# A long convolution beside an MLP: the filter in the inputs' time layout, gate weights ahead of a convolution input, and a resplit opening

## The chip, the cores and the metric

The program runs on 1 core of one Trainium2 chip. Times are device microseconds (us) of that core; the lower, the better. Every kernel was timed several times, beside runs of the kernel before on the same chip. All runs compared here are fast ones (granted clock 0.998 to 1.0).

## The reference

The output and all gradients of one layer, with S = 2048, D = 1024, F = 3584, in bf16:

```
xn  = layernorm(x)                                  # x is A_q
kv  = shift4(k) * v                                 # 4 taps along time
y   = irfft(rfft(kv, 2S) * rfft(h, 2S))[:S]         # h is ssm_k [D, S]
out = x + xn * (y + kv * ssm_D) + (relu(xn @ Wg) * (xn @ Wu)) @ Wd
returns out and the nine gradients, for a given grad_out
```

## The kernel before

TensorE is the engine that everything waits for. Most of its work is the MLP: matmuls of 128x512, each starting 0.216 us after the last. The convolution ("branch A") works on 8 groups of 128 channels. Its pieces are dealt out into the MLP's stream of matmuls: every 1760 ns of TensorE work there is a slot, and in each slot a generator of the branch may put in one piece for TensorE, with ScalarE copying the result, and one for VectorE.

Of a group, the parts that matter here are these. The gradient times xn (`gt`) and the filter (`hn`) each get their first Fourier step. `gt` comes in time layout: partition 64u + q, row r holds time 32q + 16u + r. The filter comes by channels, so TensorE transposes it first; 16 transposes take every 16th time step:

```python
    def h_tile(self, st):
        hT = self.ttile("hT")
        hv = st["hn"][:].rearrange("p r c -> p (r c)").rearrange("p (q r) -> p r q", r=16)
        pst = self.ps.tile([P, 16, P], BF16, name="pst", tag="aps")
        for r in range(16):
            self.pri.now()
            self.pri.pin(self.nc.tensor.transpose(pst[:, r, :], hv[:, r, :], self.identA[:]))
        self.act(hT[:, 0:16, :], pst[:])
        return hT
```

Here the two halves of time (u) are interleaved over the partitions, so the first Fourier step of the filter needs a table of its own, RH, of which half the entries are zeros:

```python
    def fwd1_filter(self, st, hT):          # the filter: 4 slots of 2 matmuls, full height
        ...
        for r0 in range(0, NB1, 8):
            for jj in range(2):
                r = r0 % 16 + 4 * jj
                self.mm(ps[:, 512 * jj:512 * jj + 512], self.RH[:, r0 // 16]..., hT[:, r:r + 4, :]...)
            self.act(B[:, :, r0:r0 + 8, :], ...)
            yield

    def fwd1(self, st, key, src):           # all other inputs: 2 slots of 4 matmuls, 64 rows each
        ...
        for r0 in range(0, 16, 8):
            for j in range(r0, r0 + 8, 4):
                for u in range(2):
                    rows = slice(64 * u, 64 * u + 64)
                    self.mm(ps[:, u]..., self.R[rows]..., src[rows, j:j + 4, :]...)
                self.act(B[:, :, :, j:j + 4, :], ...)
            yield
```

The loads of the branch's first group, and the slots in which it begins (`yield n` lets n ns of TensorE work pass; a slot is a pair of what goes to TensorE and to VectorE):

```python
    def steps(self):
        ...
        yield 13000
        self.load_xn(nx)       # xt: xn in time layout, from xn_d in DRAM, in pieces of 256 bytes
        self.load_taps(nx)     # skb
        self.pin = False
        yield 9000
        self.pri.strict = True
        hT = self.h_tile(nx)
        ...
    def slots(self, st, hT, gi):
        ...
        yield f1h, (lambda: self.gate_grad(st)) if gi == 0 else None     # gt = gt * xt
        yield f1h, tk
        yield f1h, self.both(lambda: self.add_D(st), tk)
        yield f1h, tk
```

The opening normalizes x in chunks of 1, 1, 1, 1, 2, ... tiles of 128 rows, so chunk 4 holds tiles 4 and 5. ScalarE sums the rows and the squares, VectorE subtracts and scales, TensorE transposes a tile into PSUM (the buffer that its results land in), VectorE copies it out as `xnT`, and the gate matmuls of that tile can start. 24 warm-up matmuls come before. The loads are issued by one queue, in this order:

```python
    load(4)
    first.append(b.row_block_T(B_W_down, 0, "wdT", 2))
    goT = [b.load_T(g, i, "goT", 8 + i) for i in range(2)]   # transposing loads
    load(5)                                                 # layer-norm chunk 5: tiles 6 and 7
```

## Time and profile before

| | before |
|---|---|
| time, median of 3 runs | 1922.31 us (1921.58 to 1922.76) |
| profiled execution | 1920.26 us, span 1918.5 us, clock 1.0 |
| TensorE busy | 1909.4 us of the span, 100% when rounded |
| VectorE, ScalarE busy | 47%, 33% |
| TensorE's waits named by the profile | about 5 us in all, 1.6 of them for gate weights |

The lines that this rests on stand in the prediction below. As there, costs are taken from the start of one block of matmuls to the start of the next, not from printed durations.

### The profile page before, as it was taken

What the parts mean: (1) busy time and instruction counts of PE and PEld (TensorE: products, weight loads), DVE (VectorE), ACT (ScalarE), POOL (GpSimd) and SP (SyncE); (2) the same over time, 40 slices, a digit from 0 to 9 for tenths busy, and PEclk for the clock granted to TensorE, in tenths of its full rate; (3) what the DMA queues carried; (4) which work ended last, traced back from release to release, by engine and by line L of the source; (5) the groups of instructions that cost most, each with busy time, mean ns of one, the idle gap of its engine ahead of it and who ended that gap; (6) DMA issues with size and microseconds to landing.
All of it is one profiled execution on the core that took longest, in us unless ns stands there. A gap on an engine that the chain in (4) does not pass through costs nothing.

```text
span 1918.5 us, 36320 instructions
## 1 busy us (share of the span) xinstructions
PE 1909.4 (100%) x15582; PEld 886.9 (46%) x15582; DVE 910.2 (47%) x1364; ACT 635.8 (33%) x867; POOL 15.7 (1%) x38
## 2 busy tenths in 40 slices
PE   9999999999999999999999999999999999999999
PEld 4444444444444444444444444444444544444444
DVE  6767767767777754534444354310122232222222
ACT  5854354364364354354344344321000000000000
POOL 1100000000000000000000000000000000000000
PEclk9999999999999999999999999999999999999999
DMA  9975778974874982645663633385999964554553
GB/s 249 276 179 144 178 185 183 221 189 133 186 187 134 248 225 78 175 128 183 158 163 92 170 100 122 100 203 209 257 240 254 235 157 121 121 121 121 121 121 72
DMA packets 628002, 323.16 MB, mean 168 GB/s; under 512 B 458360, under 2 KB 597376, under 8 KB 627840
## 3 DMA queue, kind: packets, MB, share of 16 engines
q1 hardware_dynamic: 617344, 299.99, 64.1%
q10 hardware_dynamic: 9216, 16.65, 2.9%
q0 software_dynamic: 1280, 4.20, 0.7%
q8 instruction: 122, 2.00, 0.4%
q14 instruction: 40, 0.33, 0.1%
HBM read 143.79 MB, written 95.44 MB: 125 GB/s over the span
## 4 chain that ended last, share of the span: by engine, by line
PE 96%; DVE 1%; ACT 1%; DMA 1%; issue 0%; POOL 0%; SPq 0%; ACTq 0%; POOLq 0%
PE ps_x L1283 20%; PE ps_w L1056 20%; PE ps_o L1214 10%; PE ps_h L805 9%; PE ps_u L805 9%; PE ps_g L805 9%; PE ps_d L1056 9%; PE ps L72 7%; PE ps_d L1069 1%; PE ps_w L1069 1%; ACT ln_j L743 1%; PE ps_warm L851 0%; PE pst L308 0%; PE ps_r L1244 0%; DMA wg<-in_B_W_gate_dram 0%
## 5 line engine op out<-in xcount | busy, mean ns | idle before, releaser
L1056 PE MATMUL ps_w<-ugs,xn_nat 128*128 128x512 bf16 x1728 | 383.9, 379 | 0.0
L805 PEld LDWEIGHTS <-xnT 128*128 128x128 bf16 x1792 | 170.2, 98 | 212.0 <-issue 10.2
L1056 PEld LDWEIGHTS <-xn_nat 128*128 128x128 bf16 x1728 | 164.9, 98 | 199.4 <-issue 5.5
L805 PE MATMUL ps_g<-wg,xnT 128*128 128x512 bf16 x896 | 207.0, 379 | 3.2 <-DMA wg<-in_B_W_gate_dram 1.6
L1301 ACT ACTIVATE w<-xn,m 128x512 f32<-128x512 bf16 x32 | 24.3, 806 | 553.0 <-issue 317.2
L805 PE MATMUL ps_u<-wu,xnT 128*128 128x512 bf16 x896 | 207.0, 379 | 0.5 <-ACT gh L975 0.4
L805 PE MATMUL ps_h<-wdT,goT 128*128 128x512 bf16 x896 | 206.1, 379 | 0.0
L1283 PE MATMUL ps_x<-wgT,ggT 128*128 128x512 bf16 x896 | 198.6, 379 | 0.0
L1283 PE MATMUL ps_x<-wuT,guT 128*128 128x512 bf16 x896 | 198.6, 379 | 0.0
L1214 PE MATMUL ps_o<-wd,hT 128*128 128x512 bf16 (+1 forms) x896 | 187.6, 372 | 0.0
L1056 PE MATMUL ps_d<-g_nat,hs 128*128 128x512 bf16 x768 | 172.1, 379 | 0.0
L1283 PEld LDWEIGHTS <-guT 128*128 128x128 bf16 x896 | 87.7, 98 | 105.7
L1283 PEld LDWEIGHTS <-ggT 128*128 128x128 bf16 x896 | 87.7, 98 | 105.5
L1214 PEld LDWEIGHTS <-hT 128*128 128x128 bf16 x896 | 87.7, 98 | 99.9
L805 PEld LDWEIGHTS <-goT 128*128 128x128 bf16 x896 | 85.2, 98 | 102.6 <-issue 2.9
L319 DVE STREAM_TRANSPOSE flp<-C 128x1024 f32<-128x1024 f32 x48 | 90.5, 1930 | 83.4 <-ACT C L76 83.4
L908 DVE SCALAR_TENSOR_TENSOR ru<-ru,ps_u 128x512 bf16<-128x512 bf16 x112 | 76.5, 683 | 108.6 <-issue 43.3
L975 ACT CAST gh<-ps_h 128x512 bf16<-128x512 f32 x112 | 65.4, 585 | 164.1 <-PE ps_h L805 154.8
L1160 ACT CAST wi<-ps_w 128x512 bf16<-128x512 f32 x108 | 63.6, 589 | 161.8 <-PE ps_w L1056 150.1
L76 ACT CAST C<-ps 128x1024 bf16<-128x1024 f32 x96 | 92.5, 1015 | 69.1 <-PE ps L72 68.1
L319 DVE STREAM_TRANSPOSE flp<-B 128x1024 f32<-128x1024 f32 x48 | 90.8, 1939 | 48.6 <-ACT B L76 48.6
L1056 PEld LDWEIGHTS <-hs 128*128 128x128 bf16 x768 | 72.7, 98 | 88.9 <-issue 4.2
(175 smaller groups left out, 1482.6 us busy)
## 6 DMA issues: line engine op xcount, KB each, us to landing
ug_d<-ru SPq DMA_DIRECT2D x112, 256.0 KB, 3.6
ugs<-ug_d SPq DMA_DIRECT2D x112, 256.0 KB, 4.4
wg<-in_B_W_gate_dram SPq DMA_DIRECT2D x56, 256.0 KB, 4.7
wu<-in_B_W_up_dram SPq DMA_DIRECT2D x56, 256.0 KB, 4.8
h_d<-ht SPq DMA_DIRECT2D x112, 128.0 KB, 3.6
hs<-h_d SPq DMA_DIRECT2D x56, 256.0 KB, 5.1
out_dram<-wi SPq DMA_DIRECT2D x56, 256.0 KB, 2.5
gt<-in_grad_out_dram SPq DMA_DIRECT2D x32, 256.0 KB, 4.0
```

Source lines behind the costliest of these rows:

```text
L72: self.pri.pin(self.nc.tensor.matmul(out, lhsT=lhsT, rhs=rhs, start=start, stop=stop))
L76: self.pri.pin(self.nc.scalar.copy(out=out, in_=in_))
L319: self.pri.pin(self.nc.vector.transpose(out=df[:, c0:c0 + 32, :], in_=sf[:, c0:c0 + 32, :]))
L805: self.pri.pin(self.nc.tensor.matmul(ps[:], lhsT=xT[:, kt * P:(kt + 1) * P], rhs=w(kt), start=(kt == 0), stop=(kt == self.DT - 1)), always ...
L908: self.pri.pin(nc.vector.scalar_tensor_tensor(out=ru[s][:, 1, :], in0=ru[s][:, 0, :], scalar=0.0, in1=ps[:], op0=ALU.is_gt, op1=ALU.mult))
L975: self.pri.pin(nc.scalar.copy(out=gh[:], in_=ps[:]))
L1056: self.pri.pin(self.nc.tensor.matmul(ps[:], lhsT=lhsT(st), rhs=rhs(st), start=(st == 0), stop=(st == self.ST - 1)))
L1069: self.pri.pin(self.nc.tensor.matmul(ps[i][:], lhsT=lhsT(i, st), rhs=rhs(i, st), start=(st == 0), stop=(st == self.ST - 1)))
L1160: self.pri.pin(nc.scalar.copy(out=wo[0][:, d, :], in_=ps[:]))
L1214: nc.tensor.matmul(ps, lhsT=hT[:, kt, :], rhs=self.wd[:, kt, oc], start=(kt == 0), stop=(kt == self.FT - 1))
L1283: nc.tensor.matmul(ps, lhsT=T[:, kt, :], rhs=W[:, kt, oc], start=(i == 0), stop=(i == n - 1))
L1301: nc.scalar.activation(out=w[:, oc], in_=xn[:, oc], func=ACT.Identity, scale=m[:, 7:8], bias=m[:, 6:7])
```

## The change

It has three intents. **The filter in the time layout of the other inputs**: with time half u on partitions 64u to 64u+63, the filter's first Fourier step can use `fwd1` and the table R, in 2 slots rather than 4, and RH with its zeros goes. For that, each transpose becomes two of 64 weight columns. **Gate weights ahead of xt** in the DMA queue, since TensorE had been waiting for them, with the first reader of xt moved to a later slot. **The opening split over ScalarE and VectorE**, with fewer warm-up matmuls.

```diff
@@ h_tile
-        hv = st["hn"][:].rearrange("p r c -> p (r c)").rearrange("p (q r) -> p r q", r=16)
+        hv = st["hn"][:].rearrange("p r c -> p (r c)").rearrange("p (q u r) -> p u r q", u=2, r=16)
         for r in range(16):
-            self.pri.pin(self.nc.tensor.transpose(pst[:, r, :], hv[:, r, :], self.identA[:]))
+            for u in range(2):
+                self.pri.pin(self.nc.tensor.transpose(pst[64 * u:64 * u + 64, r, :], hv[:, u, r, :], self.identA[:]))
@@ fwd1_filter and the table RH are deleted
@@ steps
-        self.load_xn(nx)
         self.load_taps(nx)
+        yield 9500
+        self.load_xn(nx)
         self.pin = False
-        yield 9000
@@ slots
-        f1h = self.fwd1_filter(st, hT)
+        f1h = self.fwd1(st, "Bh", hT)
-        yield f1h, (lambda: self.gate_grad(st)) if gi == 0 else None
+        yield f1h, tk if gi == 0 else None
+        yield None, tk
         yield f1h, tk
-        yield f1h, self.both(lambda: self.add_D(st), tk)
-        yield f1h, tk
-        yield None, tk
+        yield None, (lambda: self.gate_grad(st)) if gi == 0 else tk
+        yield None, self.both(lambda: self.add_D(st), tk)
@@ layer_norm: chunk 1's squares half on ScalarE, half on VectorE; instructions kept in program
@@ order; chunk 4's subtractions later ... (cut)
@@ flip_xn
-            copied = self.nc.vector.tensor_copy(out=xT[...], in_=pst[...])
+            copy = self.nc.scalar.copy if st == 0 and k0 == 0 else self.nc.vector.tensor_copy
+            copied = copy(out=xT[...], in_=pst[...])
@@ hidden
-                self.warm(24)
+                self.warm(17)
... (the calls that advance the layer norm are regrouped; cut)
```

More of the change, by code (lines that the diff above doesn't have):

```diff
@@ L122, in tables @@
         self.R = con.tile([P, 2, 2, NB1], BF16, name="R")
-        self.RH = con.tile([P, 2, 2, 2, NB1], BF16, name="RH")
         self.RB = con.tile([P, 64], BF16, name="RB")
@@ L147, in tables @@
         n1 = pbit(63, 1.0, "n1p")
-        n1h = pbit(126, 0.5, "n1h")
-        up = pbit(1, 1.0, "up")
         def first(n, name):
@@ L160, in first @@
             return tr
-        tr = first(n1h, "H")
-        nup = lin(up, -1.0, 1.0, "nup")
-        for u, mu in ((0, nup), (1, up)):
-            V.tensor_scalar(out=self.RH[:, u], in0=tr[:], scalar1=mu[:], scalar2=None, op0=ALU.mult)
         tr = first(n1, "R")
@@ L303, in h_tile @@
         hT = self.ttile("hT")
-        hv = st["hn"][:].rearrange("p r c -> p (r c)").rearrange("p (q r) -> p r q", r=16)
+        hv = st["hn"][:].rearrange("p r c -> p (r c)").rearrange("p (q u r) -> p u r q", u=2, r=16)
         pst = self.ps.tile([P, 16, P], BF16, name="pst", tag="aps")
         for r in range(16):
-            self.pri.now()
-            self.pri.pin(self.nc.tensor.transpose(pst[:, r, :], hv[:, r, :], self.identA[:]))
+            for u in range(2):
+                self.pri.now()
+                self.pri.pin(self.nc.tensor.transpose(pst[64 * u:64 * u + 64, r, :], hv[:, u, r, :], self.identA[:]))
         self.act(hT[:, 0:16, :], pst[:])
@@ L320, in flip @@
             yield
-    def fwd1_filter(self, st, hT):
-        B = st["Bh"] = self.big.tile([P, 64, NB1, 2], BF16, name="B", tag="big")
-        for r0 in range(0, NB1, 8):
-            ps = self.ps.tile([P, 1024], F32, name="ps0", tag="aps")
-            for jj in range(2):
-                r = r0 % 16 + 4 * jj
-                self.mm(ps[:, 512 * jj:512 * jj + 512], self.RH[:, r0 // 16].rearrange("p e a l -> p (e a l)"),
-                        hT[:, r:r + 4, :].rearrange("p r c -> p (r c)"))
-            self.act(B[:, :, r0:r0 + 8, :], ps[:].rearrange("p (r cp i) -> p cp r i", r=8, i=2))
-            yield
     def add_D(self, st):
         for rows in (slice(0, 32), slice(64, 96)):
-            b0 = st["Bh"][rows, :, 0, :]
+            b0 = st["Bh"][rows, :, 0, 0, :]
             self.tt(b0, b0, st["sD"][rows].rearrange("p (cp i) -> p cp i", i=2), ALU.add)
@@ L485, in steps @@
         yield 13000
+        self.load_taps(nx)
+        yield 9500
         self.load_xn(nx)
-        self.load_taps(nx)
         self.pin = False
-        yield 9000
         self.pri.strict = True
@@ L541, in slots @@
         tk = self.taps(st, ksh, kp, [(3, 0), (2, 1), (1, 2), (0, 3)])
-        f1h = self.fwd1_filter(st, hT)
+        f1h = self.fwd1(st, "Bh", hT)
         f1g = self.fwd1(st, "Bg", gt)
-        yield f1h, (lambda: self.gate_grad(st)) if gi == 0 else None
+        yield f1h, tk if gi == 0 else None
+        yield None, tk
         yield f1h, tk
-        yield f1h, self.both(lambda: self.add_D(st), tk)
-        yield f1h, tk
-        yield None, tk
-        flH = self.flip(st, "fH", st["Bh"][:])
+        yield None, (lambda: self.gate_grad(st)) if gi == 0 else tk
+        yield None, self.both(lambda: self.add_D(st), tk)
+        flH = self.flip(st, "fH", st["Bh"][:].rearrange("p cp u r i -> p cp (u r) i"))
         yield f1g, flH
@@ L737, in layer_norm, with half @@
             b = lambda i: smb[:, i, 0:n]
-            cut = D // 2 if i == 0 else D
+            def half(k):
+                return D // 2 if i == 0 or i == 1 and k == 2 else D
             def row_sums(j, k, func):
+                cut = half(k)
                 jk = jpool.tile([P, D], BF16, name="ln_j", tag=jtag)
@@ L746, in row_sums @@
                     if func is ACT.Square:
-                        V.tensor_tensor_reduce(out=jk[:, cut:D], in0=xt[:, j, cut:D], in1=xt[:, j, cut:D], scale=1.0,
-                                               scalar=0.0, op0=ALU.mult, op1=ALU.add, accum_out=sm[:, k + 6, 0:1])
+                        sq = V.tensor_tensor_reduce(out=jk[:, cut:D], in0=xt[:, j, cut:D], in1=xt[:, j, cut:D],
+                                                    scale=1.0, scalar=0.0, op0=ALU.mult, op1=ALU.add,
+                                                    accum_out=sm[:, k + 6, 0:1])
+                        if i == 1:
+                            self.tc.keep_in_program_order(self.ln_act)
+                            self.tc.keep_in_program_order(sq)
                     else:
@@ L753, in average @@
             def average(k, out):
-                if cut < D:
+                if half(k) < D:
                     return V.tensor_scalar(out=out, in0=f(k), scalar1=sm[:, k + 6, 0:1], scalar2=1.0 / D, op0=ALU.add,
@@ L760, in layer_norm @@
                 total = row_sums(j, 0, ACT.Copy)
-                if i != 3 and i >= 1 and j == 0:
+                if i >= 1 and j == 0:
                     self.tc.keep_in_program_order(total)
@@ L764, in layer_norm @@
             V.tensor_copy(out=f(1), in_=b(0))
+            if i == 4:
+                yield
             for j in range(n):
-                V.tensor_scalar(out=xt[:, j, :], in0=xt[:, j, :], scalar1=sm[:, 1, j:j + 1], scalar2=None,
-                                op0=ALU.subtract)
+                centred = V.tensor_scalar(out=xt[:, j, :], in0=xt[:, j, :], scalar1=sm[:, 1, j:j + 1], scalar2=None,
+                                          op0=ALU.subtract)
+                if i == 4:
+                    self.tc.keep_in_program_order(centred)
+                if i == 1:
+                    yield
                 row_sums(j, 2, ACT.Square)
@@ L838, in flip_xn @@
                                                       self.ident[:]), always=True)
-            copied = self.nc.vector.tensor_copy(out=xT[:, k0 * P:(k0 + h) * P],
-                                                in_=pst[:, k0:k0 + h, :].rearrange("p a b -> p (a b)"))
+            copy = self.nc.scalar.copy if st == 0 and k0 == 0 else self.nc.vector.tensor_copy
+            copied = copy(out=xT[:, k0 * P:(k0 + h) * P], in_=pst[:, k0:k0 + h, :].rearrange("p a b -> p (a b)"))
             if st < 4:
@@ L928, in first_gate_up @@
                 yield from step()
-                if sp == 0:
-                    next(ln)
-                    next(ln)
-                    next(ln)
                 def mid():
@@ L938, in mid @@
                     if sp == 2:
-                        chunk(2)
+                        chunk(3)
                 up(sp, mid)
@@ L1003, in hidden @@
                 flip(1)
+                for _ in range(4):
+                    next(ln)
                 yield from first_gate_up(0)
```

## The prediction

> **What bounds the kernel now.** I read the page's first, second and fourth parts first. TensorE carries nearly everything: in the busy line it covers all but 9 us of the 1918.5 us span, and in the chain that ended last it has 96%.
>
> ```profile
> PE 1909.4 (100%) x15582; PEld 886.9 (46%) x15582; DVE 910.2 (47%) x1364; ACT 635.8 (33%) x867; POOL 15.7 (1%) x38
> ...
> PE 96%; DVE 1%; ACT 1%; DMA 1%; issue 0%; POOL 0%; SPq 0%; ACTq 0%; POOLq 0%
> ```
>
> So only two kinds of time are for sale: TensorE's own work, and the few places where TensorE waits. A saved microsecond on VectorE or ScalarE is worth nothing unless TensorE waits for it. The second reading is the list of TensorE's waits in the whole run (total, times, longest).
>
> ```profile
> PE ps_g L805 <- DMA wg<-in_B_W_gate_dram: 1.6, 1, 1.6
> PE ps_warm L851 <- POOL warm L848: 1.5, 1, 1.5
> PE ps_g L805 <- DVE xnT L839: 1.0, 2, 0.7
> PE ps_u L805 <- ACT gh L975: 0.4, 1, 0.4
> ...
> ```
>
> With two of 0.3 and 0.2 left out here that is 5 us in all, and it understates: a matmul's duration (379 ns for 128x512) contains pipeline latency, while a stream of them starts one every 216 ns (16 matmuls from 85.07 to 88.53 us are 3.46 us). From here on I therefore count from start to start, in the timeline of TensorE, and not in busy time. Around the one large wait:
>
> ```profile
> 94.25 1.19 PE L308 MATMUL pst<-ident,hn 128*128 128x128 bf16 x16
> 95.27 1.89 PE L805 MATMUL ps_u<-wu,xnT 128*128 128x512 bf16 x8
> 97.39 0.59 PE L72 MATMUL ps<-hT,RH 128*128 128x512 bf16 x2 [0.23 <-ACT hT L76]
> 97.82 1.89 PE L805 MATMUL ps_h<-wdT,goT 128*128 128x512 bf16 x8
> ...
> 101.70 0.59 PE L72 MATMUL ps<-hT,RH 128*128 128x512 bf16 x2
> 103.91 2.79 PE L805 MATMUL ps_g<-wg,xnT 128*128 128x512 bf16 x8 [1.61 <-DMA wg<-in_B_W_gate_dram]
> 106.53 0.59 PE L72 MATMUL ps<-hT,RH 128*128 128x512 bf16 x2
> ...
> 110.51 0.60 PE L72 MATMUL ps<-gt,R 64*128 64x512 bf16 x4
> 111.05 1.90 PE L805 MATMUL ps_u<-wu,xnT 128*128 128x512 bf16 x8
> ```
>
> The reader should see two things. From 101.70 to 106.53 TensorE starts 2 + 8 matmuls, worth 10 x 0.216 = 2.16 us, in 4.83 us: **2.67 us lost**, more than the 1.61 us that the wait view names, because each of the four gate weight tiles arrives late in turn. And four 64-row matmuls (gt) take 111.05 - 110.51 = 0.54 us, hardly more than two full-height ones (97.82 - 97.39 = 0.43 us): they run in pairs.
>
> **What the Trainium skill says.** "TensorE: Matmul & The Clock Gate", Part 3 (Packing small matmuls), says that matmuls on different row groups or column groups run at once, each starting about 4 ns after the last. The trace agrees: within a gt pair the starts are 3 ns apart, and the pairs 229 ns. "TensorEngine Tiling (Array Packing)", Tiling Modes, Key Properties, says that a change of tiling mode drains TensorE. The trace shows what that costs: the eight full matmuls ahead of the gt block, from 108.69 us, take 110.51 - 108.69 = 1.82 us in place of 8 x 0.216 = 1.73, and the block takes 0.54 in place of 2 x 0.216 = 0.43; with 0.01 more behind it, about **0.21 us for going in and out**. The same page, Tile-to-Partition Mapping, Restrictions, says that column tiling switches off the fast weight load. No run yet shows what that means for this transpose; it is my largest doubt. The skill's page on the clock gate, Part 1, says that TensorE starts at half clock and rises after about 3.4 us of activity. Here it starts one warm-up matmul per 427 ns until 7.43 us and one per 216 ns after that, some 6 us after the first at 1.48 us. So the seven warm-up matmuls taken out are full-speed ones, and the clock should already be up when real work comes.
>
> **Part 1, the filter's first step.** Before, each of the 8 channel groups did 8 full-height matmuls (4 blocks of 2, half of the table RH being zeros): 8 x 0.216 = 1.73 us, without a mode change. After, it does what gt does: 8 matmuls of 64 rows in 2 blocks of 4, each 0.43 + 0.21 = 0.64 us, so 1.29 us. Saving 0.44 x 8 = **3.5 us**, all on TensorE, which has no slack. ScalarE copies the same four 128x1024 results, now two per slot in every second slot, as for gt, which has no TensorE wait in the list.
>
> **Part 2, the price: the filter's transpose.** To get the time layout, 16 transposes of 128x128 become 32 with 64 weight columns each, in two column groups. The 16 take 95.27 - 94.25 = 1.02 us, 64 ns each; those of xn take 56 ns (13.13 to 13.58 for 8), so reading hn with a step of 16 elements costs 8 ns. The 32 should pair up to 16 x 64 ns, plus one entry and exit. For that the model is the column-tiled tap sums:
>
> ```profile
> 196.52 1.08 PE L72 MATMUL ps<-kp,gks 128*32 128x128 bf16 x64
> ```
>
> 64 of them, four at a time, take 1.01 us (the next block starts at 197.53): 16 x 56 ns and 0.12 for leaving, plus 0.09 for entering. So even without the fast load, 128 contiguous weight columns come in within 56 ns. I take 16 x 64 ns + 0.22 = 1.24 us against 1.02: 0.22 x 8 = 1.8 us lost; at 56 ns per pair it would be 0.8. I choose **1.5 us lost**. Parts 1 and 2 together: 2.0 us gained.
>
> **Part 3, gate weights ahead of xt.** The issue order on the DMA queue explains the 2.67 us:
>
> ```profile
> 94.86 1.86 SPq L88 DMA_DIRECT2D xt<-xn_d  x2
> ...
> 98.89 2.28 SPq L798 DMA_DIRECT2D wg<-in_B_W_gate_dram  x4
> ```
>
> xt must wait until the last layer-norm chunk has landed in xn_d (94.71 us), and the queue is in order, so wg leaves at 98.89 and its first tile is there at 103.9, 5 us later; skb and two ug_d stores stand between. In the changed program's order on that engine, skb, two ug_d stores and wg come first, then an h_d store, xt and wu. The gate matmuls that wg replaces finish near 91.8 us, and the ug_d stores wait for products that VectorE ends at 94.3; so wg leaves between 92.5 and 94.5 and lands by 97.5 to 99.5, where TensorE asks for it at about 102. The **2.67 us** go. xt now lands near 102 to 103; its only reader, the product with gt, was moved from the first slot to the fourth (about 102.5), and its result is wanted near 109. wu, behind xt, leaves at about 98 and lands from 103 to 105.5; it is asked for from 105 to 106.5: tight, not late. One table set, RH, falls away too, with one ScalarE table load of 1.28 us; the stall of 0.54 us at 91.8 (up matmuls waiting for a gh copy behind two table loads and a sine) should mostly go, but a similar sequence in the new ScalarE order, ahead of another gh copy, could cost some of it. I count 0.3. Sum of part 3: **3.0 us**.
>
> **Part 4, the opening.** Before, the transposes could start at 7.9 us, when the first normalized half is ready, but the 24 warm-up matmuls hold TensorE until 9.6. With 17 they end 7 x 0.216 = 1.5 us earlier, near 8.1. ScalarE and VectorE each copy a half; the gate matmuls start near 9.2 in place of 10.53. But this moves the limit to the layer norm of the next tiles, which the change speeds up less. Before, the gate matmuls of tiles 0 to 3 start at 10.53, 14.53, 19.00 and 23.79, the last after a copy by VectorE:
>
> ```profile
> 23.79 1.90 PE L805 MATMUL ps_g<-wg,xnT 128*128 128x512 bf16 x8 [0.71 <-DVE xnT L839]
> ```
>
> Following the new order on each engine with the durations of this trace (square over half a row 0.69 on VectorE, seven small VectorE steps at 0.2 each, scaling 0.49, copy 0.69) I get these four starts at about 9.2, 13.8, 18.5 and 23.0. From the fourth on TensorE runs without gaps in both. So of the 1.3 us won at the first tile **0.8 us** stay. The last is won by copying tile 3 out of PSUM ahead of two subtractions of chunk 4 (0.88 us), which stood before it.
>
> **Sum.** 2.0 + 3.0 + 0.8 = 5.8 us. 1922.3 - 5.8 = **1916.5 us**, 0.3%.
>
> **Rivals.** (a) The transposes without fast weight load do not pair, or their strided loads double: 32 x 64 ns is 2.05 us + 0.22 per group, 10 us lost, so part 2 eats everything: 1922 to 1925. For it: hn's loads take 148 ns where contiguous ones take 98. Against it: the tap sums. (b) wg's wait is replaced by one for wu or for ScalarE's gh copies, in the same 20 us: 1 to 2 us come back, 1918. For it: wu's margin is under 1 us. (c) The layer-norm chain eats the opening's whole gain, or the warm-up cut brings half clock back: 1917.5. For it: chunk 3's subtraction now comes after a copy and a product on VectorE. (d) The transposes are as cheap as the tap sums and the stall at 91.8 goes whole: 1915.5.
>
> **Range and chances.** Parts 1 and 3 are read off measured blocks and I trust them to 0.5 us each; part 2 has a long tail upwards, part 4 is good to 0.5. Runs spread by 1.2 us. So 1913.5 to 1919.5. Nothing here reaches 2% (38 us): same 0.99.
>
> **What would show it.** In the new timeline: filter blocks of four at 64x512 taking 0.54 us up to the next full matmul; the transpose block near 1.1 us (wrong if over 1.6); no gap over 0.3 us ahead of the gate matmuls near 102 us; the fourth gate block near 23.0 us. The prediction falls if TensorE shows a new wait of over 1 us after 30 us, or if the transposes run singly.

## The result, and the profile after

| | before | after |
|---|---|---|
| time, median | 1921.94 us (4 runs, 1919.28 to 1922.76) | 1922.08 us (4 runs, 1921.34 to 1923.36) |
| ratio of after to before | | 1.0004, 95% interval 0.9986 to 1.0021 |
| span of the profiled execution | 1918.5 us | 1920.2 us |

A ratio, here and below, is the mean time of one kernel's fast runs over the mean time of the other's fast runs of the same rounds, so it isn't quite the ratio of the medians. No gain is measured: 1922.08 us lies outside the predicted 1913.5 to 1919.5. The outputs are correct.

The changed kernel is bound as before; its busy line, and the chain that ended last:

```profile
PE 1890.6 (98%) x15465; PEld 885.7 (46%) x15703; DVE 908.9 (47%) x1355; ACT 633.1 (33%) x866; POOL 15.0 (1%) x37
...
PE 97%; issue 1%; DVE 1%; DMA 1%; ACT 0%; SPq 0%; DVEq 0%; ACTq 0%
```

The 19 us less of TensorE time are no gain. There are 15703 weight loads, and each belongs to one matmul, yet only 15465 matmuls are recorded: 238 records are missing from this trace, and the "issue" in the chain fits that (a missing record of 0.216 us leaves a hole of about 0.16). Starts are therefore the only safe measure. The list of TensorE's waits (total, times, longest), with the "issue" rows left out:

```profile
PE ps_g L801 <- DVE xnT L836: 2.4, 2, 2.1
...
PE ps_warm L847 <- POOL warm L844: 1.5, 1, 1.5
...
PE pst_x L833 <- DVE ln_x L783: 1.2, 2, 1.0
```

The wait for gate weights has gone from the list, and a wait of 2.1 us for a copied tile of xn is new. Next the stretch of TensorE's timeline (start, duration, work) that answers to the one shown of before:

```profile
94.39 2.00 PE L302 MATMUL pst<-ident,hn 128*64 128x128 bf16 x32
96.32 1.90 PE L801 MATMUL ps_u<-wu,xnT 128*128 128x512 bf16 x7
98.34 0.61 PE L72 MATMUL ps<-hT,R 64*128 64x512 bf16 x4
98.89 3.63 PE L801 MATMUL ps_h<-wdT,goT 128*128 128x512 bf16 x16
102.44 0.60 PE L72 MATMUL ps<-hT,R 64*128 64x512 bf16 x4
102.98 3.63 PE L801 MATMUL ps_g<-wg,xnT 128*128 128x512 bf16 x16
```

Three things are to be seen. The filter's matmuls take 102.98 - 102.44 = 0.54 us per block of four, as predicted. The gate matmuls at 102.98 run without a gap. But the transposes, 1.02 us before, hold TensorE from 94.39 to 96.32, that is 1.93 us, and they do so in each of the 8 groups. They do run in pairs: in the trace's own start times the two halves of a pair start 0 to 9 ns apart in every group. But the next pair starts 110 to 114 ns later, where the prediction had 64.

The opening, in the same view of before and then of after. The lines are the last four matmuls of a down-gradient tile (`ps_h`) and the gate matmuls of tile 4 (in after, those of tile 3 first):

```profile
30.74 1.03 PE L805 MATMUL ps_h<-wdT,goT 128*128 128x512 bf16 x4
31.62 3.63 PE L805 MATMUL ps_g<-wg,xnT 128*128 128x512 bf16 x16
```

```profile
22.60 1.90 PE L801 MATMUL ps_g<-wg,xnT 128*128 128x512 bf16 x7 [0.29 <-DVE xnT L836]
...
29.54 1.03 PE L801 MATMUL ps_h<-wdT,goT 128*128 128x512 bf16 x4
32.70 3.63 PE L801 MATMUL ps_g<-wg,xnT 128*128 128x512 bf16 x15 [2.13 <-DVE xnT L836]
```

After leads by 23.79 - 22.60 = 1.19 us at tile 3 and by 1.20 us at the `ps_h` block; at tile 4 it waits, and is 1.08 us behind.

**The whole account**, from start to start on TensorE, after minus before:

| part | us |
|---|---|
| 8 transpose blocks: 8.11 us in all before, 15.45 after, with 0.09 for entering the narrower mode and 0.01 behind it each | +8.2 |
| filter matmuls: 32 pairs of 0.432 before; 16 blocks of 0.538, with 0.096 for entering and 0.01 behind each | -3.5 |
| wait for gate weights near 102 us | -2.7 |
| three small stalls before it, at 58, 81 and 92 us (tile 4's start to the first transposes: 62.63 us, then 61.69) | -0.9 |
| wait for the copied filter transpose | -0.2 |
| a stall at 539 us, in before alone (cause not looked for) | -0.3 |
| opening, up to tile 4 (31.62, then 32.70) | +1.1 |
| sum (the spans differ by 1.7) | +1.7 |

(The sixth block of after is printed as 2.15 us, but the matmul behind it, at 823.54 us, is one of the missing records: its weight load is there. One start of 0.216 is taken off for it.)

### The profile page after: what moved, and what is told of

It reads as the page before. It is cut to its first block, busy times and chain, and to the rows that moved or that the text cites. A ratio compares the mean times of both kernels' runs of the same rounds, so it can differ in the third digit from the quotient of the medians.

```text
span 1920.2 us, 36321 instructions
## 1 busy us (share of the span) xinstructions
PE 1890.6 (98%) x15465; PEld 885.7 (46%) x15703; DVE 908.9 (47%) x1355; ACT 633.1 (33%) x866; POOL 15.0 (1%) x37
## 4 chain that ended last, share of the span: by engine, by line
PE 97%; issue 1%; DVE 1%; DMA 1%; ACT 0%; SPq 0%; DVEq 0%; ACTq 0%
PE ps_x L1277 20%; PE ps_w L1050 19%; PE ps_u L801 10%; PE ps_g L801 10%; PE ps_h L801 10%; PE ps_o L1208 10%; PE ps_d L1050 9%; PE ps L72 6%; PE ps_d L1063 1%; PE pst L302 1%; DMA ln_x<-in_A_q_dram 0%; PE ps_w L1063 0%; PE ps_r L1238 0%; DMA ugs<-ug_d 0%; PE pst_x L833 0%
## 5 line engine op out<-in xcount | busy, mean ns | idle before, releaser
L1050 PE MATMUL ps_w<-ugs,xn_nat 128*128 128x512 bf16 x1671 | 376.3, 380 | 5.3 <-issue 3.5
L801 PE MATMUL ps_g<-wg,xnT 128*128 128x512 bf16 x864 | 202.3, 380 | 5.6 <-DVE xnT L836 2.4
L801 PE MATMUL ps_h<-wdT,goT 128*128 128x512 bf16 x865 | 201.3, 380 | 2.7 <-issue 1.6
L1050 PE MATMUL ps_d<-g_nat,hs 128*128 128x512 bf16 x739 | 167.2, 380 | 3.3 <-issue 2.7
```

What stands on the lines that cost most here:

```text
L801: self.pri.pin(self.nc.tensor.matmul(ps[:], lhsT=xT[:, kt * P:(kt + 1) * P], rhs=w(kt), start=(kt == 0), stop=(kt == self.DT - 1)), always ...
L1050: self.pri.pin(self.nc.tensor.matmul(ps[:], lhsT=lhsT(st), rhs=rhs(st), start=(st == 0), stop=(st == self.ST - 1)))
```

## The experiments

Two things had to be explained: why the transposes cost double, and where the opening's gain went. Unless it is said otherwise, a kernel was timed in five rounds and gave the right result. The kernels that read wrong columns of the filter give a wrong result: only their times count. One idea fell before any run: a single transpose whose 128 weight columns are fetched by a pattern of two levels (u, then q) doesn't build, since the build asks for exactly one free dimension in the stationary operand, the one that is loaded as weights.

### One part of the change at a time

Before plus the filter part alone (`h_tile`, `fwd1` for the filter, RH gone, the new slots with `gate_grad` kept in the first):

```diff
+        hv = ....rearrange("p (q u r) -> p u r q", u=2, r=16)     # and the 32 half transposes
-        f1h = self.fwd1_filter(st, hT)
+        f1h = self.fwd1(st, "Bh", hT)
```

> The kernel before with the filter part alone (time layout, 32 half transposes, 8 tiled matmuls per group); opening and load order as before. Transpose theory (the 32 half transposes run one after another, 1.93 us plus 0.1 for entering, against 1.01, as the trace of the changed kernel shows): 8 x 1.02 lost, 8 x 0.44 won, so 4.5 us slower than the kernel before (range 3.5 to 5.5). The prediction's parts 1 and 2: 2.0 us faster.

Measured: 1922.63 us (1921.21 to 1923.35) beside 1922.13 of before, ratio 1.0002 [0.9988, 1.0016]. In TensorE's timeline of this kernel the first transpose block starts at 94.68 and the next matmul at 96.61: 1.93 us, with nothing else of the change in the kernel. So the cost belongs to the filter part. By the account above this part loses 8.2 - 3.5 = 4.7 us of TensorE's time; some of it hides, since the wait for gate weights shrank to 0.98 us when TensorE came to it later. The time alone wouldn't have shown the loss: its interval reaches from -2.3 to +3.1 us. (The expectation's "one after another" is a misreading: here too the starts come in pairs, 0 to 9 ns apart, and 110 to 114 ns from pair to pair.)

Before plus the load order alone:

```diff
-        self.load_xn(nx)
         self.load_taps(nx)
+        yield 9500
+        self.load_xn(nx)
-        yield 9000
# and gate_grad moved from the first to the fourth slot
```

> The kernel before with the load order alone (gate weights ahead of xt, gate_grad in the fourth slot). Both theories: the 2.67 us around 102 us go, the rest stays, so 2.5 to 3 us faster. Rival: a later wait, for wu or for the product of gt and xt, takes their place: 0 to 1 us faster.

Measured: 1919.51 us (1917.74 to 1921.88), ratio 0.9988 [0.9976, 1.0001]; the interval just reaches 1. The timeline of the profiled execution:

```profile
104.90 3.62 PE L805 MATMUL ps_g<-wg,xnT 128*128 128x512 bf16 x16
108.35 0.59 PE L72 MATMUL ps<-hT,RH 128*128 128x512 bf16 x2
108.78 4.16 PE L805 MATMUL ps_u<-wu,xnT 128*128 128x512 bf16 x16
```

The 16 gate matmuls start one per 0.216 us (108.35 - 104.90 = 3.45 us), so the wait is gone. By itself that proves little: chunk 5 of the layer norm came late in this execution (see the next run), TensorE began the transposes at 97.03 us, 2.8 later than before, and would have had less to wait for in any case. The cleaner witness is `contig_halves`, below, which has the same load order: TensorE comes to these matmuls at 100.90 us, 1.2 earlier than before (102.13), and runs all 16 in 3.46 us. In `full_strided`, also at 100.90, a wait of 0.64 us for `wg` comes back, so the margin is small. And the up matmuls behind them, 4.16 us rather than 3.62, wait 0.55 us in the kernel with the load order alone, for their weights `wu`: the wait has partly moved on.

Before plus the opening alone (the hunks of `layer_norm`, `flip_xn` and `hidden`):

> The kernel before with the opening alone (17 warm-up matmuls, split squares, copy by ScalarE, other order of the chunks). Theory of the late chunk: the gate matmuls of tile 4 wait for copies that VectorE makes behind chunk 5, whose load sits behind transposing loads in the queue, so the first four tiles start up to 1.3 us earlier and the gain is gone at tile 4: 0 to 1.2 us slower than before. The prediction's part 4: 0.8 us faster.

Measured: 1922.72 us (1920.00 to 1924.35), ratio 1.0001 [0.9989, 1.0014]. Its profile happens to be the fair comparison for the opening. ScalarE's timeline for the first row sum of chunk 5 (in brackets the idle time ahead of it, and what ended it), in before, in after and in this kernel:

```profile
26.85 1.06 ACT L743 ACTIVATE ln_j<-ln_x 128x1024 bf16<-128x1024 bf16 x1 [0.53 <-DMA ln_x<-in_A_q_dram]
```

```profile
27.93 1.06 ACT L729 ACTIVATE ln_j<-ln_x 128x1024 bf16<-128x1024 bf16 x1 [2.07 <-DMA ln_x<-in_A_q_dram]
```

```profile
26.89 1.06 ACT L746 ACTIVATE ln_j<-ln_x 128x1024 bf16<-128x1024 bf16 x1 [0.88 <-DMA ln_x<-in_A_q_dram]
```

In all three, ScalarE waits for the DMA that brings chunk 5. And tile 4's gate matmuls start 4.77 us after this sum, in all three: 31.62, 32.70, and 31.66 in the opening-only kernel, where TensorE sat idle for 0.94 us before it.

With the chunk at the same moment (26.85 and 26.89), the old opening and the new one reach tile 4 at the same moment (31.62 and 31.66). In before TensorE comes there just as the copies end, without an idle gap. What the new opening wins on tiles 0 to 3 it waits away here. Why tile 4, of chunk 4, hangs on the load of chunk 5 is seen in VectorE's timeline of the changed kernel:

```profile
30.15 0.17 DVE L747 TENSOR_SCALAR ln_b<-ln_s 128x2 bf16<-128x2 f32 x1 [1.78 <-ACT ln_j L729]
...
30.56 0.88 DVE L758 TENSOR_SCALAR ln_x<-ln_x,ln_s 128x1024 bf16<-128x1024 bf16 x2
31.36 0.68 DVE L968 TENSOR_TENSOR ru<-ru,gh 128x1024 bf16<-128x1024 bf16 x1
31.96 1.28 DVE L836 COPY xnT<-pst_x 128x1024 bf16<-128x1024 bf16 x2
```

The copies of `xnT` at 31.96 empty the PSUM tiles of tiles 4 and 5, which TensorE transposed from 28.65 to 29.54; their data had lain ready for over two microseconds. But in this trace VectorE takes its instructions in the program's order. Ahead of them stand the average and the subtraction of chunk 5, which wait 1.78 us for ScalarE's sums, which wait for the DMA; and the product with `gh`, whose copy on ScalarE stands behind the same sums.

The moment of this load varies from profile to profile: in the 16 profiles (before and after among them) of kernels that keep its place in the queue, the first sum of chunk 5 starts between 26.18 and 29.00 us, and tile 4 starts 4.77 to 4.88 us after it. That is up to 2.8 us of difference between two executions. It is likely a source of the spread in all the timings here; only one execution of each kernel has a trace, so this isn't shown.

### The opening's floor moved

The changed kernel, with chunk 5 loaded ahead of two transposing loads of the gradient:

```diff
-    goT = [b.load_T(g, i, "goT", 8 + i) for i in range(2)]
     load(5)
+    goT = [b.load_T(g, i, "goT", 8 + i) for i in range(2)]
```

> The changed kernel with the load of layer-norm chunk 5 issued ahead of the first two transposing loads of grad_out. Theory of the late chunk: the wait of TensorE ahead of the gate matmuls of tile 4 (2.1 us in the changed kernel's profile) goes, these start near 30.5 us in place of 32.7: 1 to 2 us faster than the changed kernel and less spread. Rival: the chunk is not what they wait for, or the transposing loads now come late themselves: no change.

Measured: 1922.37 us (1920.62 to 1926.16), ratio 1.0011 [0.9999, 1.0023]. Tile 4 starts at 31.04 us, with 0.33 us idle just before it instead of 2.13, so the theory of the wait holds. The time doesn't move. TensorE's waits name one reason, up matmuls near 106 us waiting for their weights:

```profile
PE ps_u L801 <- DMA wu<-in_B_W_up_dram: 1.5, 2, 1.1
```

TensorE, being earlier, runs into a second floor: `wu` stands behind xt, and comes no earlier. So xt was also moved behind `wu`, from its own load point into the second slot:

```diff
-        self.load_xn(nx)
         self.pin = False
...
-        yield None, tk
+        yield (lambda: self.load_xn(st)) if gi == 0 else None, tk
```

> The changed kernel with the first xt load behind the up weights too. Theory of the two floors: in the traces of the changed order the up matmuls near 105 us wait up to 1.5 us for wu tiles, which leave the queue 3 us late behind xt; this goes. But the opening's wait for chunk 5 stays and differs from run to run: 0.5 to 1.5 us faster than the changed kernel. Rival: VectorE, which now waits longer for xt, stalls TensorE: no gain or a loss.

> wu_first together with early_ln5, both floors away. Theory of the two floors: alone, early_ln5 gained nothing because TensorE, earlier at the end of the opening, waited for wu; together they give 2 to 3.5 us against the changed kernel, near 1919. Rival (the early chunk does harm elsewhere, as its slow runs suggest): no better than wu_first.

Measured, `wu_first` (this alone): 1921.5 us (1921.09 to 1923.27), ratio 1.0006 [0.9994, 1.0019]. `wu_early` (this and the earlier chunk 5): 1922.35 us (1921.07 to 1923.85), ratio 1.0009 [0.9996, 1.0021]. The queue's own timeline, of after and then of `wu_first`:

```profile
96.67 1.92 SPq L88 DMA_DIRECT2D xt<-xn_d  x2
98.69 4.11 SPq L794 DMA_DIRECT2D wu<-in_B_W_up_dram  x4
```

```profile
96.41 2.87 SPq L793 DMA_DIRECT2D wu<-in_B_W_up_dram  x4
99.60 1.37 SPq L88 DMA_DIRECT2D xt<-xn_d  x2
```

Behind xt, the four issues of `wu` take 4.11 us and end at 102.80; ahead of it they take 2.87 us and end at 99.28, and no wait for `wu` near 106 us is left in `wu_first` or in `wu_early` (which has another, of 0.36 us, at 61.22). That the small pieces of xt are what slows the issues behind it isn't shown: no run loads xt in larger ones. In `wu_early` tile 4 starts at 30.88 us. Yet the expected gain did not come: in its profile TensorE's last block starts at 1909.22 us, 1.34 us earlier than in after (1910.56), but the span ends 11.35 us behind that, not 9.65. The extra 1.7 us lie behind the issue of the last store (1915.98 us); in the other 19 profiles the span ends 3.63 to 3.74 us after TensorE's last start, here 5.35. So one execution's end hides the lead in the profile; why the five rounds show none is open. What is shown is that both floors exist and can be moved; that moving them pays in time is not shown.

### The transposes

Same kernel as after, with only the columns changed that the half transposes read, to adjacent ones (wrong result):

```diff
-    transpose(pst[64 * u:64 * u + 64, r, :], hv[:, u, r, :], ...)
+    transpose(pst[64 * u:64 * u + 64, r, :], st["hn"][:, r, 64 * u:64 * u + 64], ...)
```

> The changed kernel with each of the 32 half transposes reading 64 neighbouring elements of a row in place of 64 elements 64 bytes apart (wrong filter on purpose: the result that depends on it is wrong). If the stride is what costs[...]: the block falls from 1.93 us to about 1.0 (16 x 56 ns + 0.12) and the kernel gains 7 us on the changed one. If half transposes do not pair whatever they read: block stays near 1.9 us and the time stays.

Measured: 1916.44 us (1915.91 to 1919.62), ratio 0.9974 [0.9962, 0.9987], a block 1.02 us:

```profile
93.22 1.08 PE L302 MATMUL pst<-ident,hn 128*64 128x128 bf16 x32
94.23 1.90 PE L801 MATMUL ps_u<-wu,xnT 128*128 128x512 bf16 x8
```

The pairs now start 56 ns apart, in all 8 groups, in place of 110 to 114. So 32 half transposes can be had for the price of the old 16; it is the strided reading that doubles them. The next kernel goes back to 16 transposes of the full width with a step of 16, all else as after (wrong result, as R expects the other layout):

```diff
+    hv = ....rearrange("p (q r) -> p r q", r=16)
+    transpose(pst[:, r, :], hv[:, r, :], ...)
```

> The changed kernel with the 16 full 128x128 transposes of before in place of the 32 halves (wrong filter on purpose: the time order of the rows is not the one that the tiled matmuls want). Theory of the transposes: a block of 1.01 us without a mode change in place of 1.93 + 0.10, so 8 x 1.02 = 8.2 us faster than the changed kernel, 8 faster than before, near 1914. Rival (the chip lost time elsewhere and the transposes are hidden in waits): under 4 us faster.

Measured: 1914.83 us (1914.11 to 1916.45), ratio 0.9969 [0.9957, 0.9981], a block 1.00 us. Strides alone are therefore cheap too, at full width; the two together are dear. Then the step, with `hv` rearranged as `"p (a s) -> p s a"` and `hv[:, r % s, 64*u:64*u+64]` for s = 16, 8, 2 and 4, and for the full width `hv[:, r % 4, 0:128]` (all wrong):

> The changed kernel with half transposes that read elements 16 apart (32 bytes, as the full transposes of before do), in place of 32 apart (wrong filter on purpose). If the larger step is what costs: the block of 32 falls from 1.93 us to about 1.1 (16 x 64 ns + 0.1). If it is the half width[...] at any step: it stays at 1.9.

> The same with elements 8 apart (16 bytes; wrong filter on purpose). If the cost grows with the step: between 1.0 and 1.9 us. If any step costs the same: as at 16.

> The same with elements 2 apart (4 bytes; wrong filter on purpose). If the cost grows with the step: about 1.0 us. If every step other than one costs the same: as at 16.

> The changed kernel with its 32 half transposes reading weight columns 4 elements (8 bytes) apart; the result is wrong on purpose. Known by now: step 1 and 2 take 1.02 us per group, steps 8, 16 and 32 take 1.93 to 2.08 us. Theory line rule (the Trainium skill, "SBUF — State Buffer", on its lines of 16 bytes: two accesses in one line are enough for full bandwidth): at step 4 there are two elements in each line, so the block takes 1.02 us and LDWEIGHTS 110 ns, as at step 2. Rival gradual: the cost grows with the bytes spanned, and the block lies between, near 1.5 us.

> The changed kernel with 16 full transposes of 128 weight columns 4 elements apart; the result is wrong on purpose. Known: contiguous 0.89 us per group and 98 ns for one LDWEIGHTS, step 16 1.00 us and 148 ns. Theory line rule: as contiguous, near 0.90 us and 98 ns, so that step 16 pays for its lines too, only little. Rival: every strided full-width load costs the same, 1.00 us and 148 ns.

The view of one tile, here `hn`, has its weight loads with min, median and maximum in ns. First after itself (step 32), then steps 8, 4 and 2:

```profile
L302 PEld LDWEIGHTS <-hn x256: 185/204/209, 94.4 to 1118.4; 128*64 128x64 bf16 x128
```

```profile
L302 PEld LDWEIGHTS <-hn x256: 192/217/218, 93.3 to 1118.5; 128*64 128x64 bf16 x128
```

```profile
L302 PEld LDWEIGHTS <-hn x256: 135/143/159, 93.1 to 1111.6; 128*64 128x64 bf16 x128
```

```profile
L302 PEld LDWEIGHTS <-hn x256: 107/110/110, 96.0 to 1115.0; 128*64 128x64 bf16 x128
```

And the full width, with step 16 in before, and step 4:

```profile
L308 PEld LDWEIGHTS <-hn x128: 142/148/164, 94.0 to 1116.4; 128*128 128x128 bf16 x128
```

```profile
L301 PEld LDWEIGHTS <-hn x128: 111/113/115, 93.4 to 1111.1; 128*128 128x128 bf16 x128
```

| step, in elements | bytes | elements in 16 bytes | half width: block, load | full width: block, load |
|---|---|---|---|---|
| 1 | 2 | 8 | 1.02 us, 110 ns | 0.89 us, 98 ns |
| 2 | 4 | 4 | 1.02 us, 110 ns | |
| 4 | 8 | 2 | 1.11 us, 143 ns | 0.89 us, 113 ns |
| 8 | 16 | 1 | 2.07 us, 217 ns | |
| 16 | 32 | 1 | 2.08 us, 218 ns | 1.00 us, 148 ns |
| 32 | 64 | 1 | 1.93 us, 204 ns | |

(Blocks are medians of the 8 groups. The single runs took, for half widths with steps 16, 8, 4 and 2, 1922.88, 1922.11, 1915.21 and 1918.68 us, and 1914.5 for the full width with step 4; one run each. The 3.5 us between steps 2 and 4 are mostly the opening's and what follows it: the first transposes start at 96.00 and 93.14 us. The contiguous full width is from the kernels of the next section.) The step from 4 to 8 elements is the edge, and from there on the step hardly matters. The Trainium skill, "SBUF — State Buffer", in the section "Door 1: The DMA port swizzle", has a note that puts the edge there: SBUF, the memory that the weights are read from, has lines of 16 bytes, two accesses within a line are enough for full bandwidth, and each access that crosses into a new line pays. For the half-width loads this case agrees on the edge: at one element per line the block costs 89% to 104% more than contiguous. It doesn't agree that two are quite enough: there the block costs 9% more (1.11 for 1.02 us) and a load 143 ns for 110, where the expectation had no loss. For full-width loads it agrees only in small: one element per line costs 1.00 for 0.89 us. So that the lines are the cause is argued from the place of the edge. A reason why the full-width load pays less would be the "fast weight load", which "TensorEngine Tiling (Array Packing)", Tile-to-Partition Mapping, Restrictions, says is off in column tiling; it fits these numbers, but no run here switches that mode by itself. Nor does any run read a strided half alone, without its pair running beside it. What is shown is that half width in pairs and a step of 8 elements or more are dear together, and neither alone.

The rivals that fell are: that half transposes don't pair (the two start 0 to 9 ns apart, strided or not), that the larger step of 32 is to blame (steps 8 and 16 cost as much or more), and that the cost rises gradually with the step (an edge between 4 and 8).

### A version that keeps the idea

If the weights must be contiguous, another engine can reorder the filter first, and TensorE does 16 full transposes of adjacent columns. By VectorE, one copy of about 1.89 us per group, in the slot where the transposes had stood, these being moved to a later one:

```diff
+    hv = ....rearrange("p (q u r) -> p r u q", u=2, r=16)
+    self.vcopy(hp[:].rearrange("p r (u q) -> p r u q", u=2), hv)
-            for u in range(2):
-                transpose(pst[64 * u:64 * u + 64, r, :], hv[:, u, r, :], ...)
+            transpose(pst[:, r, :], st["hp"][:, r, :], ...)
```

> The changed kernel, made right in another way: VectorE first copies hn into the order r, u, q, so that 16 full transposes read 128 neighbouring elements. Correct results. Transposes at 56 ns: block 0.90 us, no mode change, 8 x 1.13 = 9.0 us faster than the changed kernel, near 1913. The copies (estimated 1 to 2.2 us each on VectorE, which has slack) should cost nothing; if they delay VectorE's copies that free PSUM, 1 to 3 us come back as new waits of TensorE.

> Both of the above together, a candidate that should beat both kernels: 9.0 + 1.5 = 10.5 us faster than the changed kernel, near 1911.5, 0.5% under the kernel before. If the gains do not add, 1913.

Measured, `dve_reorder`: 1916.75 us (1915.97 to 1917.75), ratio 0.9978 [0.9966, 0.9989], with 1.0 us of new waits for the reordered tile and 1.5 us for `wu`. `dve_early` (with the earlier chunk 5): 1917.71 us (1915.73 to 1923.37, 6 runs), ratio 0.9989 [0.9975, 1.0002]; it waits 3.1 us for `wu`.

Then with xt behind `wu`, and the reorder on ScalarE, two halves of 1.97 us in slots that had no copy for it (the first group's by VectorE), in the buffer of xt, as a buffer of its own didn't fit into SBUF:

```diff
+        yield None, lambda: next_reorder(0, 8)     # two slots of the group before
...
+        yield lambda: next_reorder(8, 16), qh
```

> wu_first, and the filter's reorder done by ScalarE in two halves long before it is needed (by VectorE for the first group), then 16 full transposes of neighbouring elements. Block 0.90 us without a wait: 9.0 + 1 us faster than the changed kernel, near 1912. dve_reorder lost some to TensorE's waits for the copy; if ScalarE's copies delay its PSUM copies instead, 1914 to 1916.

> act_wu with the early chunk 5: all three. Theory: 9.0 + 2 to 3.5, so 1909 to 1911. If the early chunk does harm, 1912 or more and a wider spread than act_wu.

> act_wu with the opening of the kernel before (24 warm-up matmuls and all the rest of it). If the new opening gains nothing, because tile 4 waits for chunk 5 in both: the same as act_wu, 0.998 of the kernel before. If the opening gained 0.8 us that other losses hid: 0.8 us slower than act_wu (which five rounds can't show, but the start of tile 4's gate matmuls in the trace can).

| kernel | median us | ratio to before |
|---|---|---|
| `act_wu` | 1915.71 (1914.91 to 1919.04) | 0.9979 [0.9965, 0.9993] |
| `act_wu_early`: and chunk 5 earlier | 1915.88 (1912.02 to 1920.41) | 0.9974 [0.9961, 0.9988] |
| `act_wu_oldopen`: `act_wu` with the opening of before | 1913.97 (1913.67 to 1914.99) | 0.9962 [0.9948, 0.9975] |

TensorE's timeline of `act_wu_oldopen`:

```profile
93.85 1.06 PE L306 MATMUL pst<-ident,hp 128*128 128x128 bf16 x16
94.75 1.89 PE L796 MATMUL ps_u<-wu,xnT 128*128 128x512 bf16 x7
```

The block takes 0.90 us, less than the 1.02 of before. This version is faster than before by 0.4% (1913.97 beside 1921.77 in the same rounds); beside after it wasn't timed, but after takes the time of before. With the old opening or with the new one, timed in different calls, the intervals overlap, so the new opening is again worth nothing that these runs can show.

## Why the prediction was wrong

**Part 1, the filter's first step: right.** 3.5 us predicted, 3.5 found, by the blocks that it named: four 64x512 matmuls in 0.54 us. (One reading is off, and nothing hangs on it: in a gt block the second pair starts 225 ns behind the first, not 229.)

**Part 2, the price: the step that failed.** "The 32 should pair up to 16 x 64 ns": they do pair, but a pair takes 110 to 114 ns and not 64. So the price is 8.2 us where 1.5 were put down, and that is 6.7 of the 7.5 us between the predicted sum (-5.8) and the found one (+1.7). The model for the pairing, the tap sums, had contiguous weights of 32 columns, and the half transposes read one element every 64 bytes; the analogy carried over the mode of the array but not the access pattern. The sign was there to read: hn's loads took 148 ns where contiguous ones took 98, and the text put that down as 8 ns on a transpose and kept it as a small additive cost. The second half of rival (a) is what happened: strided loads that double, 2.05 us per block against the 1.93 found, and a time of 1922 to 1925. Its first half, no pairing, isn't, and its reason, the missing fast load, stays argued. This rival was given too little weight.

**Part 3, gate weights ahead of xt: right, and a little more.** The 2.67 us went, with the queue's order as foretold (`wg` leaves at 93.07 us). The stalls before it gave 0.9 instead of 0.3. Rival (b), a new wait for `wu`, is real but hid: it shows where TensorE comes to its up matmuls sooner behind the last issue of `wu`: 3.1 us behind it with the load order alone (0.55 us lost), 2.4 in `early_ln5` (1.5 lost), 3.6 in after (none). In the changed kernel the slow transposes and the late tile 4 kept TensorE just late enough; that is luck, and so is part of the clean result here (0.64 us for `wg` are back in `full_strided`).

**Part 4, the opening: failed at its last step.** The first four tiles came as predicted or better: 9.05, 13.42, 17.83 and 22.60 us, against 9.2, 13.8, 18.5 and 23.0. But "From the fourth on TensorE runs without gaps in both" doesn't hold for the new opening: tile 4 is tied to the landing of chunk 5, and the lead is lost. In the two profiles it even turned to +1.1 us; `opening_only`, with the chunk at the same moment as before, shows zero. So rival (c)'s first half is what happened, by a load and not by the subtraction that it named.

**What it said would prove it wrong** did: a transpose block over 1.6 us, and a new wait over 1 us after 30 us. The third sign, transposes that run singly, did not appear. That after comes out level with before, to 0.2 us in the medians, is a cancelling of gains and losses.

## What to carry to other kernels

Before a wide transpose is cut into narrow ones, compare the bytes between neighbouring weight columns: narrow loads with less than two elements in 16 bytes cost twice as much here as contiguous ones, and it was cheaper to let an idle engine make the columns contiguous. When a wait on the critical engine is removed, follow the first instructions behind it to the next thing that they need, down to the DMA that brings it; here two leads of a microsecond ended at loads that had been just in time (chunk 5, then `wu`). And model a block by one that has its access pattern as well as its tile shape.

## What the Trainium skill lacked or had wrong

- "TensorEngine Tiling (Array Packing)", Tile-to-Partition Mapping, Restrictions, says that column tiling switches off the fast weight load, but not what strided weights then cost. Here a pair of transposes of 64 columns each takes 110 to 124 ns when the columns are 8 or more elements apart, 56 ns when they are adjacent, and one of 128 columns 56 ns adjacent, 63 ns at a step of 16.
- "SBUF — State Buffer", Door 1: The DMA port swizzle, has the note on lines of 16 bytes without a time and without a word on weight loads, and holds two hits per line to be enough. Here a half-width load took 110 ns at 4 or 8 elements in a line, 143 at two, and 204 to 218 at one; a full-width one 98 ns at 8, 113 at two and 148 at one.
- "TensorEngine Tiling (Array Packing)", Tiling Modes, Key Properties, says that a mode switch drains TensorE and gives no cost. Here it was about 0.09 to 0.10 us to enter a block of narrower tiles and 0.11 us to leave it.
- "TensorE: Matmul & The Clock Gate", Part 4 (PE-mode transpose), gives about 275 ns for a 128x128 transpose in a kernel. Here 16 in a row take 0.89 us, one per 56 ns; only the single printed duration (219 ns) is of that size.
- No page was found that says what a load in small pieces does to the loads behind it in the queue: four loads of 256 KB took 4.11 us to issue behind xt, in 256-byte pieces, and 2.87 us ahead of it; whether the pieces or the bytes do it isn't shown.
